# Memory rows and riding rows by DMA in place of selection matmuls, with a fixed TensorE order, in a recurrent attention and gated-MLP kernel

## The chip, the core and the metric

The kernel runs on one core of one Trainium2 chip. The core has five instruction queues: TensorE (PE, matmuls, with its weight loads shown as PEld), VectorE (DVE), ScalarE (ACT), GpSimd (POOL) and SyncE (SP), which issues nearly all DMAs here. The engines run side by side and wait for one another through semaphores. The metric is the device time of one execution in microseconds, lower is better; the number given is the median of several executions.

## What is computed

Two rounds of the same pair of residual blocks over x of 2048 rows by 448, in bfloat16:

```python
x = x + A(layernorm(x));  x = x + B(layernorm(x))
x = x + A(layernorm(x));  x = x + B(layernorm(x))

def A(x, mem):                      # 64 segments of 32 rows, one after the other
    for s in range(64):
        h = concat([mem, x[32*s:32*s+32]])          # 8 memory rows + 32 rows = 40
        q, k, v = h @ Wq, h @ Wk, h @ Wv            # 16 heads of 256
        p = softmax(mask(q @ k.T / 16))             # every row sees the memory rows
        o = (p @ v) @ Wo
        mem = o[:8]                                 # the next segment's memory
        out.append(o[8:])
def B(x):                           # ReGLU: 448 -> 1792 -> 448
    return (relu(x @ W_gate) * (x @ W_up)) @ W_down
```

The memory makes A a recurrence: segment s+1 can't begin its queries of the memory rows before segment s has its eight new ones.

## The kernel before

**Algebra.** A setup of about 72 us folds the weights: for each head, M = Wq·Wk transposed (448 by 448) and N = Wv·Wo (448 by 448), both kept in SBUF (`Mw`, `M3`, `Nw`). A head's scores are then h·M·h transposed, and its output is p·h·N. The 448 columns are cut into three chunks of 128 and one of 64, so 16 heads make 56 blocks of N.

**Steps.** The two rounds (layer 0 and layer 1) are interleaved with a lag of four segments: step t, for t from 0 to 67, does segment t of layer 0 and segment t-4 of layer 1 in the same instructions where it can (one half of the partitions, or one half of the columns, for each). A step consists of these groups, named as in the code:

- `m_nat`: brings the new memory rows in natural layout into hK; also moves the "riding" rows (below)
- `t_block`: h·M for all heads (three blocks of matmuls; the copies out are `t_copies`, into TTm for the memory queries and TTs for the segment queries)
- `s_mem`, `p_t_mem`, `u_mem`, `un_mem`: scores, softmax, transposed probabilities, p·h (copied into UTm) and ·N for the memory rows; the result is `mv`, which holds the new memory rows and, in a second set of 16 columns of its window, rows that came along
- `m_t`: the new memory rows, transposed, into hT (the keys of the next step)
- `s_seg`, `seg_pt`, `u_seg`: the same for the 32 segment rows; the transposed probabilities PTs come by a transposing DMA
- every second step `un` (·N, and the residual into XB), `ln_b` with a transposing DMA to xBT, `b_layer` and `b_down` (the MLP), and `ln_a`, with a transposing DMA to xAT, for a later pair of segments

hK holds h in natural layout (rows on partitions): 32 segment rows and 8 memory rows for each layer and each of four slots. `u_mem` and `u_seg` read it, over all 40 rows. "Riding" rows are the segment rows of one layer-1 segment that went through `un_mem` beside the memory rows, in columns of UTm; they come out in `mv` and have to be added into the residual XB, 16 rows at a time.

**How mv gets where it is needed, before.** `mv` has 64 rows of 224 columns: the two column halves of 32 result rows. `m_nat` (L1207) does two matmuls with 0/1 matrices `seln`, prepared in setup (L712, L730), which put the rows onto the partitions at which hK, and the riding rows, are wanted; hK is then copied out of PSUM (L867 on ScalarE or L868 on VectorE), and the riding rows go into XB in two VectorE additions, one in each of two steps (L1225 into part, L1228 into XB). `m_t` does 14 small matmuls with `selm`, one VectorE copy and two ScalarE copies into hT.

**What sets the order.** All operations are recorded first (`_Order.add`), with what they read and write. `_Order.run` then lays them out on the five queues: whenever an engine is free in its account, it takes, among the operations that can start soonest, the one with the highest priority. The priority of a TensorE group comes from a table, `SLOT` (L174), by name, index and step: steps 0 to 3 and 64 to 67 have entries of their own, the steps between share one set for each step number modulo four, shifted by `PERIOD`. Other operations take theirs from what depends on them, plus `BIAS` (L164). The result is a fixed order on each engine, and every engine executes its queue in order; waits are added in `_Sched._need` (L69). Four steps with t % 4 = 0 to 3 are called a group of four here, and its first to fourth step.

**Tile shapes.** Matmuls here use TensorE whole (128 rows by 128 columns), in quarters of 64 by 64, or in column groups of 32, and the order decides how often the shape changes from one group to the next. A group with `alt=2`, such as m_nat, may be issued whole or in four column groups, whichever fits its neighbour.

Of the kernel before, what the change touches and what calls it, by code (L numbers as in the profile page):

```python
# [9 lines left out]
ALU = mybir.AluOpType  # L10
AX = mybir.AxisListType

D = 448
# [3 lines left out]
MEM = 8  # L17
SEG = 32
KEYS = SEG + MEM

NSEG = 64
# [3 lines left out]
DH = D // 2  # L25
# [4 lines left out]
LAG = 4  # L30
# [15 lines left out]
class _Sched:  # L46
# [118 lines left out]
    "t_blockm+": 5039, "t_blocks+": 3092, "s_mem+": -5347, "p_t_mem+": -85965, "u_mem+": -33073, "un_mem+": -7892,  # L165
    "un_memh+": -922, "m_t+": -4047, "m_tk+": 22842, "s_seg+": -67106, "seg_pt+": 139, "u_seg0+": -1085,
    "u_seg1+": -443, "u_seg2+": -2585, "u_seg3+": 51857, "m_nat+": 3185, "t_block0f+": 662, "t_block0r+": 9055,
    "t_block1r+": 5367, "t_block2r+": 47616, "ln_a+": 3189, "ln_ac+": -12510, "un+": -111, "ln_b+": -12694,
    "b_layer+": -12996, "b_down+": -5101, "m_natx+": -272, "stay": 46, "win": 118,
# [5 lines left out]
    "t_block0f.0@a0": 38481, "t_block0r.0@a0": 67520, "t_block0r.1@a0": 67619, "t_block0r.2@a0": 67659,  # L175
    "t_block0r.3@a0": 67621, "t_block0r.4@a0": 67623, "t_block0r.5@a0": 70316, "t_block1f.0@a0": 38479,
    "t_block1r.0@a0": 67656, "t_block1r.1@a0": 65565, "t_block1r.2@a0": 67536, "t_block1r.3@a0": 67536,
    "t_block2r.0@a0": 74464, "s_mem.0@a0": 47525, "fills_mem.0@a0": 48698, "fills_mem.1@a0": 46922,
    "p_t_mem.0@a0": 67621, "u_mem.0@a0": 57404, "fillu_mem.0@a0": 48642, "un_mem.0@a0": 45458, "m_t.0@a0": 45462,
    "s_seg.0@a0": 67571, "u_seg0.0@a0": 57410, "u_seg1.0@a0": 57412, "u_seg2.0@a0": 53498, "u_seg3.0@a0": 57450,  # L180
    "m_nat.0@a1": 45460, "t_block0f.0@a1": 48668, "t_block0r.0@a1": 46927, "t_block0r.1@a1": 46927,
    "t_block0r.2@a1": 46949, "t_block0r.3@a1": 46923, "t_block0r.4@a1": 46925, "t_block0r.5@a1": 46921,
    "t_block1f.0@a1": 41930, "t_block1r.0@a1": 47860, "t_block1r.1@a1": 46934, "t_block1r.2@a1": 45772,
    "t_block1r.3@a1": 49346, "t_block2r.0@a1": 42010, "s_mem.0@a1": 46933, "fills_mem.0@a1": 46935,
    "fills_mem.1@a1": 46937, "p_t_mem.0@a1": 46939, "u_mem.0@a1": 55586, "fillu_mem.0@a1": 47077,
    "un_mem.0@a1": 45464, "m_t.0@a1": 45504, "s_seg.0@a1": 46931, "u_seg0.0@a1": 57408, "u_seg1.0@a1": 57416,
    "u_seg2.0@a1": 57443, "u_seg3.0@a1": 61660, "un0.0@a1": 45416, "un0.1@a1": 45474, "un0.2@a1": 45706,
    "un0.3@a1": 86975, "un1.0@a1": 45440, "un1.1@a1": 45442, "un1.2@a1": 88746, "un1.3@a1": 86915, "un2.0@a1": 89373,
    "un2.1@a1": 86931, "un2.2@a1": 45626, "un2.3@a1": 45444, "un3.0@a1": 45669, "un3.1@a1": 47005,
    "b_layerf.0@a1": -26914, "b_layer.0@a1": 46812, "b_layer.1@a1": 46814, "b_layerf.1@a1": 46769,  # L190
    "b_layer.2@a1": 46810, "b_layer.3@a1": 46826, "b_down.0@a1": 44084, "b_down.1@a1": 44185, "b_down.2@a1": 47906,
    "b_down.3@a1": 47908, "b_down.4@a1": 47910, "b_down.5@a1": 47912, "b_down.6@a1": 47914, "m_nat.0@a2": 59501,
    "t_block0f.0@a2": 20916, "t_block0r.0@a2": 59499, "t_block0r.1@a2": 59503, "t_block0r.2@a2": 59507,
    "t_block0r.3@a2": 59497, "t_block0r.4@a2": 45282, "t_block0r.5@a2": 59135, "t_block1f.0@a2": 48655,
    "t_block1r.0@a2": 59518, "t_block1r.1@a2": 59522, "t_block1r.2@a2": 59520, "t_block1r.3@a2": 59516,
    "t_block2r.0@a2": 48355, "s_mem.0@a2": 41082, "p_t_mem.0@a2": 44080, "u_mem.0@a2": 76553, "un_mem.0@a2": 45624,
    "m_t.0@a2": 45632, "s_seg.0@a2": 59497, "u_seg0.0@a2": 76181, "u_seg1.0@a2": 87512, "u_seg2.0@a2": 76188,
    "u_seg3.0@a2": 48788, "m_nat.0@a3": 70659, "t_block0f.0@a3": 47001, "t_block0r.0@a3": 46830,
    "t_block0r.1@a3": 46838, "t_block0r.2@a3": 46828, "t_block0r.3@a3": 46832, "t_block0r.4@a3": 46836,
    "t_block0r.5@a3": 46834, "t_block1f.0@a3": 47003, "t_block1r.0@a3": 48603, "t_block1r.1@a3": 48556,  # L200
    "t_block1r.2@a3": 48562, "t_block1r.3@a3": 48560, "t_block2r.0@a3": 47673, "s_mem.0@a3": 49023,
    "p_t_mem.0@a3": 46824, "u_mem.0@a3": 48389, "un_mem.0@a3": 47916, "m_t.0@a3": 47902, "s_seg.0@a3": 47542,
    "u_seg0.0@a3": -27897, "u_seg1.0@a3": -26535, "u_seg2.0@a3": -26849, "u_seg3.0@a3": -26851, "un0.0@a3": 47904,
    "un0.1@a3": 47906, "un0.2@a3": 47908, "un0.3@a3": 47910, "un1.0@a3": 44845, "un1.1@a3": 61780, "un1.2@a3": 47816,
    "un1.3@a3": 47939, "un2.0@a3": 47830, "un2.1@a3": 47904, "un2.2@a3": 47948, "un2.3@a3": 47820, "un3.0@a3": 48725,
    "un3.1@a3": 47900, "b_layerf.0@a3": -26847, "b_layer.0@a3": 132467, "b_layer.1@a3": 132469,
    "b_layerf.1@a3": -26849, "b_layer.2@a3": 132473, "b_layer.3@a3": 132471, "b_down.0@a3": 36585,
    "b_down.1@a3": 49933, "b_down.2@a3": 47822, "b_down.3@a3": 47832, "b_down.4@a3": 46594, "b_down.5@a3": 39676,
    "b_down.6@a3": 47861, "m_nat.0@0": 450296, "t_block0f.0@0": 6985, "t_block0r.0@0": 20136, "t_block0r.1@0": 20140,
    "t_block0r.2@0": 190863, "t_block0r.3@0": 20138, "t_block0r.4@0": 190282, "t_block0r.5@0": 192142,  # L210
    "t_block1f.0@0": 108960, "t_block1r.0@0": 190290, "t_block1r.1@0": 104286, "t_block1r.2@0": 190288,
    "t_block1r.3@0": 104284, "t_block2r.0@0": 190292, "s_mem.0@0": 20286, "p_t_mem.0@0": 20493, "u_mem.0@0": -63618,
    "un_mem.0@0": -180079, "m_t.0@0": -438077, "s_seg.0@0": 100996, "u_seg0.0@0": -60148, "u_seg1.0@0": -65797,
    "u_seg2.0@0": 363822, "u_seg3.0@0": 26075, "m_nat.0@1": -268008, "t_block0f.0@1": 108464, "t_block0r.0@1": 278134,
    "t_block0r.1@1": 106489, "t_block0r.2@1": 192798, "t_block0r.3@1": 278136, "t_block0r.4@1": 278138,
    "t_block0r.5@1": 273223, "t_block1f.0@1": 17227, "t_block1r.0@1": 192130, "t_block1r.1@1": 192132,
    "t_block1r.2@1": 106130, "t_block1r.3@1": 192132, "t_block2r.0@1": 106128, "s_mem.0@1": -151868,
    "p_t_mem.0@1": -65864, "u_mem.0@1": -28209, "un_mem.0@1": 311409, "m_t.0@1": 192901, "s_seg.0@1": 106134,
    "u_seg0.0@1": 22464, "u_seg1.0@1": 57795, "u_seg2.0@1": 57793, "u_seg3.0@1": 195218, "un0.0@1": 139411,
# [310 lines left out]
def MM(out, lhsT, rhs, **kw):  # L530
    return (out, lhsT, rhs, kw)
# [921 lines left out]
```

## Time and profile before

| | us |
|---|---|
| median of three runs | 1547.75 |
| lowest, highest | 1545.5, 1551.47 |
| the profiled execution | 1548.94 |
| its span, first to last instruction | 1547.1 |
| VectorE busy by DVE copies of TTs, 64x256 and 128x320 | 43.0 + 28.8 |
| ScalarE busy by copies of TTs, 128x320 | 129.7 |
| POOL busy | 111.8 |
| ACT copies into hT, 64x16 (118 of them) | 21.3 |

The page gives, for each engine, busy time and share of the span, a digit row in 40 slices, the chain of work that ended last, and groups of instructions. A group's line has the source line, engine, operation, the tile it writes and the tiles it reads, the count, and then busy time in all, mean duration in ns, and the idle time of the engine just before, with what ended it. Nearly all operations go through helpers, so L139 is every matmul, L867 every ScalarE copy and L868 every copy on VectorE or GpSimd; the tiles tell them apart. Matmuls overlap in the pipeline, so the distance between starts, and not the duration, is what one costs.

The DMA part of the page, for the transfers that are issued inside the steps (KB each, median us from issue to landing; the transposing ones have no size):

```
out_dram<-ys SPq DMA_DIRECT2D x32, 56.0 KB, 2.1
XA<-in_A_x_dram SPq DMA_DIRECT2D x28, 56.0 KB, 2.2
PTs<-Ps SPq DMA_TRANSPOSE x67, 2.6
xBT<-xn SPq DMA_TRANSPOSE x34, 3.2
```

### The profile page before, as it was taken

How to read it: one execution, taken by the hardware profiler on the slowest of the kernel's cores; microseconds unless marked ns; L12 is line 12 of the kernel's file. 1: busy time of each engine (PE TensorE's matmuls, PEld its weight loads, DVE VectorE, ACT ScalarE, POOL GpSimd, SP SyncE). 2: the span in 40 equal slices, each digit the busy share in tenths (PEclk: the TensorE clock that was granted, in tenths of full speed). 3: DMA queues.
4: the chain of work that ended last, by engine and by line, in shares of the span. 5: the costliest groups of instructions: out<-in, count | busy, mean ns of one | idle time of the engine just before them, and what ended most of it. 6: DMA issues, size and time to landing. Idle time of an engine off the chain costs nothing.

```text
span 1547.1 us, 87788 instructions
## 1 busy us (share of the span) xinstructions
PE 1489.5 (96%) x40831; PEld 1173.4 (76%) x40835; DVE 826.2 (53%) x2213; ACT 865.0 (56%) x2780; POOL 111.8 (7%) x259
## 2 busy tenths in 40 slices
PE   6989999999999999999999999999999999999998
PEld 2568777778787777878687778878777787878776
DVE  6434545555554655554564554555465555556445
ACT  5745554655555565555556465554656556555543
POOL 4000000000000000000000000000000000000000
PEclk9999999999999999999999999999999999999999
DMA  9841111000010101000010110001010111101010
GB/s 216 185 124 26 19 14 21 19 15 17 20 21 15 22 15 20 17 15 21 15 22 15 20 20 15 17 20 21 15 22 16 20 16 16 19 15 19 19 19 15
DMA packets 129757, 46.37 MB, mean 30 GB/s; under 512 B 117736, under 2 KB 129264, under 8 KB 129392
## 3 DMA queue, kind: packets, MB, share of 16 engines
q1 hardware_dynamic: 129040, 40.53, 13.6%
q8 instruction: 320, 5.24, 1.4%
q14 instruction: 45, 0.37, 0.1%
q10 hardware_dynamic: 352, 0.24, 0.1%
HBM read 10.33 MB, written 1.84 MB: 8 GB/s over the span
## 4 chain that ended last, share of the span: by engine, by line
PE 86%; ACT 4%; DVE 4%; DMA 3%; SPq 3%; issue 1%
PE b L139 86%; SPq L688 3%; DMA PTs<-Ps 2%; ACT TTs L867 1%; ACT UTm L867 1%; ACT Em L1072 1%; ACT big L867 1%; DMA xBT<-xn 1%; DVE stat L1116 1%; ACT TTm L867 0%; ACT Es L1115 0%; DMA Nw<-in_A_Wo_dram 0%; DVE UTm L868 0%; DVE Es L1114 0%; DVE xn L921 0%
## 5 line engine op out<-in xcount | busy, mean ns | idle before, releaser
L139 PE MATMUL b<-hT,Mw 128*128 128x80 bf16 (+1 forms) x11424 | 439.5, 200 | 0.6 <-issue 0.3
L139 PEld LDWEIGHTS b<-hT,Mw 128*128 128x128 bf16 x11424 | 418.7, 100 | 14.8 <-issue 1.8
L139 PE MATMUL b<-Nw,big 128*32 128x448 bf16 (+1 forms) x3324 | 294.5, 353 | 0.6 <-DMA Nw<-in_A_Wo_dram 0.5
L867 ACT ACTIVATE TTs<-b 128x320 bf16<-128x320 f32 (+5 forms) x676 | 282.1, 418 | 22.1 <-PE b L139 20.5
L867 ACT ACTIVATE TTm<-b 128x80 bf16<-128x80 f32 (+5 forms) x660 | 152.7, 232 | 181.6 <-PE b L139 175.8
L139 PE MATMUL b<-Nw,UTm 128*32 128x224 bf16 x7504 | 196.2, 262 | 17.2 <-DVE UTm L868 15.8
L139 PEld LDWEIGHTS b<-Nw,big 128*32 128x32 bf16 (+1 forms) x3324 | 133.7, 97 | 102.5 <-issue 5.8
L139 PE MATMUL b<-xBT,big 128*128 128x128 bf16 (+3 forms) x4900 | 209.5, 215 | 1.0 <-DVE xn L921 0.6
L139 PEld LDWEIGHTS b<-Nw,UTm 128*32 128x32 bf16 x7504 | 177.9, 98 | 35.7 <-DVE UTm L868 18.0
L139 PEld LDWEIGHTS b<-xBT,big 128*128 128x128 bf16 (+1 forms) x4900 | 183.2, 101 | 21.1 <-issue 8.2
L867 ACT ACTIVATE big<-b 128x512 bf16<-128x512 f32 (+1 forms) x250 | 125.4, 559 | 85.5 <-PE b L139 84.5
L139 PE MATMUL b<-hT,M 64*64 64x80 bf16 (+2 forms) x6808 | 144.1, 199 | 2.7 <-issue 1.3
L868 DVE CAST TTm<-b 64x64 bf16<-64x64 f32 (+4 forms) x224 | 49.7, 223 | 176.0 <-PE b L139 172.6
L139 PEld LDWEIGHTS b<-hT,M 64*64 64x64 bf16 (+2 forms) x6808 | 109.6, 107 | 28.3 <-ACT hT L867 11.2
L868 POOL COPY hK<-xn 32x448 bf16<-32x448 bf16 x136 | 75.2, 553 | 624.9 <-DVE xn L921 618.6
L1350 ACT ACTIVATE gT<-b 128x512 bf16<-128x512 f32 (+2 forms) x128 | 67.8, 541 | 63.7 <-PE b L139 58.0
L868 DVE CAST TTs<-b 64x256 bf16<-64x256 f32 (+5 forms) x208 | 88.9, 428 | 20.0 <-PE b L139 19.8
L139 PE MATMUL b<-big,hB 128*32 128x448 bf16 (+1 forms) x742 | 95.2, 353 | 0.5 <-DVE hB L1351 0.4
L1351 DVE TENSOR_TENSOR hB<-gT,b 128x512 bf16<-128x512 bf16 (+2 forms) x128 | 78.3, 614 | 28.3 <-PE b L139 14.4
L867 ACT ACTIVATE UTm<-b 128x448 bf16<-128x448 f32 (+2 forms) x132 | 73.3, 566 | 33.8 <-PE b L139 33.8
L867 ACT ACTIVATE sumA<-b 64x224 f32<-64x224 f32 x67 | 23.7, 354 | 122.0 <-PE b L139 122.0
L139 PE MATMUL b<-PTs,hK 40*64 40x512 bf16 (+1 forms) x1024 | 83.5, 364 | 6.5 <-DMA PTs<-Ps 6.5
(109 smaller groups left out, 1509.0 us busy)
## 6 DMA issues: line engine op xcount, KB each, us to landing
big<-in_A_Wo_dram SPq DMA_DIRECT2D x3, 896.0 KB, 5.9
out_dram<-ys SPq DMA_DIRECT2D x32, 56.0 KB, 2.1
big<-in_B_W_up_dram SPq DMA_DIRECT2D x7, 224.0 KB, 3.1
big<-in_B_W_gate_dram SPq DMA_DIRECT2D x7, 224.0 KB, 4.1
big<-in_B_W_down_dram SPq DMA_DIRECT2D x7, 224.0 KB, 2.7
XA<-in_A_x_dram SPq DMA_DIRECT2D x28, 56.0 KB, 2.2
PTs<-Ps SPq DMA_TRANSPOSE x67, 2.6
Nw<-in_A_Wo_dram SPq DMA_DIRECT2D x1, 896.0 KB, 6.1
```

Of the source, the lines that this page charges most:

```text
L139: ins = E.matmul(out, lhsT=lhsT, rhs=rhs, **kw)
L688: S.q.add("dma", ("sp",), {"sp": 6200.0 if w == "Wv" and q else 4100.0}, lambda E: E.dma_start_transpose(out=st[w, q], in_=src[w][:, q * 1 ...
L867: return E.activation(out(), src(), ACT.Copy, **({} if scale is None else {"scale": scale}))
L868: return E.tensor_copy(out(), src()) if scale is None else E.tensor_scalar(out(), src(), scale, None, op0=ALU.mult)
L1072: S.act(lambda E, i=i: E.activation(S.Em[:, i, :], src()[:, i, :], ACT.Exp, bias=st[:, 32 + i:33 + i], scale=1.0, accum_out=st[:, 34 + i:3 ...
L1116: S.dve(lambda E: E.tensor_reduce(st[:, 48:48 + n], Es, AX.X, ALU.add), w, [("Es",)], [("ss", 1)])
L1350: S.act(lambda E, g=g, R=R, n=n: E.activation(S.gT[:, g, 0:n], R[0].b()[:, 0:n], ACT.Relu), n, R[0].res(), [("gT", g)])
L1351: S.dve(lambda E, g=g, R=R, n=n, fcs=fcs: E.tensor_tensor(S.hB[:, fcs[0]:fcs[-1] + 1, 0:w], S.gT[:, g, 0:n].rearrange("p (a b) -> p a b", ...
```

## The change

1. `m_nat` has no matmul and no PSUM tile any more. The memory rows go from `mv` into hK by DMA on SP, one for each layer and column half (four per step), and the riding rows by two more DMAs into a new tile `ride`. In every second step one VectorE addition (ride + XA into XB) takes the place of the two. `seln` and its setup are gone.
2. `m_t` does 16 matmuls instead of 14, so that all 128 partitions of the last chunk are filled, and one VectorE copy into hT takes the place of three.
3. After the priorities are worked out, all TensorE groups of steps 8 to 63 that have a `SLOT` entry are sorted by it and chained one to the next, so that the plan must keep that order. The chain is in the plan alone and adds no waits.
4. `SLOT` and `BIAS` have new numbers throughout, and a cost allowance of 60 ns in `s_mem` is dropped in the plan.

```diff
@@ _Order.graph
             o.prio = -o.key
+        line = sorted((o for o in self.ops if o.slot in SLOT and 2 * LAG <= o.t < NSEG), key=lambda o: o.key)
+        for a, b in zip(line, line[1:]):
+            if a not in b.preds:
+                b.preds.append(a)
+                b.np += 1
+                a.succs.append(b)
@@ alloc
-        self.seln = self.sb("seln", [128, 2, 2, 128])
+        self.ride = self.sb("ride", [128, D])
@@ m_t
-                for g in range(4) if c < 3 else (2, 3):
-                    d = 128 * c + 32 * g - (64 if c == 3 else 0)
+                for g in range(4):
+                    d = 128 * c + 32 * (g if c < 3 else g % 2)
...
-        S.cp(lambda: S.hT[:, pp, 0:3, l0:l1, s, SEG:KEYS], lambda: v()[:, 0:3], 48, C.res(), mk[:-2], eng=("dve",))
-        S.cp(lambda: S.hT[0:64, pp, 3, l0:l1, s, SEG:KEYS], lambda: v()[64:128, 3], 16, C.res(half=(1,)), mk[-2:-1], eng=("act",), base=(64, 0))
-        S.cp(lambda: S.hT[64:128, pp, 3, l0:l1, s, SEG:KEYS], lambda: v()[64:128, 3], 16, C.res(half=(1,)), mk[-1:], eng=("act",), base=(64, 64))
+        S.cp(lambda: S.hT[:, pp, :, l0:l1, s, SEG:KEYS], lambda: C.b()[:, 0:64].rearrange("p (c l q) -> p c l q", c=4, l=2)[:, :, l0:l1, :], 64, C.res(), mk, eng=("dve",))
@@ m_nat
-        S.mm(lambda: [MM(C.b()[:, DH * j:DH * j + DH], S.seln[:, j, w, :], S.mv[:, :], start=True, stop=True) for j in range(2)],
-             2 * S.pitch(DH), [("mem",), ("sel", 0), ("sel", 1)], C.res() + [("hKm", pp, s, l) for l in ls], alt=2)
-        for l in ls:
-            r = slice(64 * l + 32, 64 * l + 40)
-            S.cp(lambda r=r: S.hK[r, pp, s, :], lambda r=r: C.b()[r, 0:D], D, C.res(half=(l,)), [("hKm", pp, s, l)], base=(r.start, r.start))
+            for n in range(2):
+                a, b = 64 * l + 32, 32 * n + 16 * w + 8 * l
+                S.qdma(f"mk{l}{n}", lambda E, a=a, b=b, n=n: E.dma_start(S.hK[a:a + 8, pp, s, DH * n:DH * n + DH], S.mv[b:b + 8, :]),
+                       [("hKm", pp, s, l, n)], [("mem",)])
...
-            if w == 0:
-                S.dve(lambda E: E.tensor_tensor(S.part[r, :], C.b()[r, 0:D], S.XA[r, p % 4, :], ALU.add), D,
-                      C.res(half=(1,)) + [("XA", p % 4, 1)], [("part", 1)], base=(64, 64))
-            else:
-                S.dve(lambda E: E.tensor_tensor(S.XB[r, (p + 1) % 2, :], C.b()[r, 0:D], S.part[r, :], ALU.add), D,
-                      C.res(half=(1,)) + [("part", 1)], [("XB", (p + 1) % 2, 1)], base=(64, 64))
+            for n in range(2):
+                a, b = 64 + 16 * w, 32 * n + 16 * (1 - w)
+                S.qdma(f"ride{n}", lambda E, a=a, b=b, n=n: E.dma_start(S.ride[a:a + 16, DH * n:DH * n + DH], S.mv[b:b + 16, :]), [("ride", w, n)], [("mem",)])
+            if w == 1:
+                S.dve(lambda E: E.tensor_tensor(S.XB[r, (p + 1) % 2, :], S.ride[r, :], S.XA[r, p % 4, :], ALU.add), D,
+                      [("ride", i, n) for i in range(2) for n in range(2)] + [("XA", p % 4, 1)], [("XB", (p + 1) % 2, 1)], base=(64, 64))
```

`qdma` records a DMA on SP's queue. `u_mem` and `u_seg` now read the memory rows of hK under two keys (one for each column half), so they wait for the DMAs that write them. In the programs as built, SP's queue has 376 more DMAs: 252 into hK and 124 into ride.

## The prediction

> **What bounds the kernel now.** I read the page first, then the windows by stage, the waits of TensorE, the groups by shape, and the timeline where TensorE stands still.
>
> ```profile
> span 1547.1 us, 87788 instructions
> ...
> PE 1489.5 (96%) x40831; PEld 1173.4 (76%) x40835; DVE 826.2 (53%) x2213; ACT 865.0 (56%) x2780; POOL 111.8 (7%) x259
> ...
> PEclk9999999999999999999999999999999999999999
> ...
> PE 86%; ACT 4%; DVE 4%; DMA 3%; SPq 3%; issue 1%
> ```
>
> TensorE is busy 96% of the span at full clock, and 86% of the chain that ended last is its own. VectorE and ScalarE are half idle. So a microsecond counts only if it leaves TensorE's queue or is a moment in which TensorE waits. The windows (length, then busy time of PE, PEld, DVE, ACT, POOL, clock, DMA share, GB/s) say where those moments are:
>
> ```profile
> 0.00:80.00 80.00, 61.70 (x672) 32.13 (x675) 45.67 (x149) 52.46 (x154) 18.67 (x32) 0.98 0.91 197
> 80.00:255.00 175.00, 162.77 (x4942) 132.07 (x4940) 85.41 (x248) 90.13 (x314) 9.25 (x24) 0.95 0.19 41
> 255.00:1490.00 1235.00, 1213.15 (x33679) 970.60 (x33677) 668.49 (x1749) 700.47 (x2237) 81.04 (x196) 1.00 0.10 18
> 1490.00:1548.00 58.00, 51.93 (x1552) 38.59 (x1552) 26.62 (x69) 21.96 (x78) 2.86 (x7) 1.00 0.08 17
> ```
>
> Setup ends near 72 us, steps 0 to 7 near 215 us; then come 14 like groups of four steps of 88.4 us each (from un_mem to un_mem in the trace). From 255 to 1490 us only 21.9 us are idle. The waits name them (total, times, longest):
>
> ```profile
> PE b L139 <- DVE UTm L868: 15.8, 15, 1.2
> ...
> PE b L139 <- DMA PTs<-Ps: 6.5, 8, 2.8
> PE b L139 <- DVE mv L1179: 3.7, 10, 0.9
> ...
> PE b L139 <- DVE Pm L1076: 2.8, 3, 1.2
> ```
>
> UTm is the large one: once in four steps.
>
> **Part 1, the selection matmuls.** The removed groups (busy, mean ns | idle before):
>
> ```profile
> L867 ACT ACTIVATE hK<-b 8x448 bf16<-8x448 f32 x111 | 59.5, 536 | 35.1 <-PE b L139 19.4 <-DVE part L1225 8.7 <-DVE XB L1228 4.7
> L1225 DVE TENSOR_TENSOR part<-b,XA 32x448 f32<-32x448 f32 x31 | 19.3, 622 | 8.5 <-PE b L139 7.9
> L139 PE MATMUL b<-mv,seln 128*128 128x224 bf16 x90 | 16.0, 260 | 0.0
> L139 PE MATMUL b<-mv,seln 128*32 128x224 bf16 x176 | 8.5, 257 | 1.0 <-DVE mv L1179 0.9
> ```
>
> The two seln rows add to 24.5 us of busy time. The Trainium skill ("Trainium Kernel Development and Optimization", Performance Expectations) calls matmul busy time a bad metric because matmuls are pipelined. Here that decides the sum, so I read start times instead:
>
> ```profile
> 837.81 0.35 PE L139 MATMUL b<-mv,seln 128*128 128x224 bf16 x2
> 838.00 2.06 PE L139 MATMUL b<-Nw,big 128*128 128x448 bf16 x10
> ```
>
> The next matmul starts 0.19 us after the first of m_nat. 67 calls x 0.19 = **-12.7 us**, not -24.5. The copies leave engines that have room: ScalarE loses 111 x 0.536 = 59.5 us, VectorE 31 x 0.622 + 15 x 0.628 = 28.7 us; worth nothing by themselves, only where they stood ahead of something TensorE waits for (part 4). The seln set-up (L712, L730) ends by about 9.4 us, while TensorE's first work waits 8.4 us for the DMA ys<-in_A_mem_dram: 0.
>
> **Part 2, m_t.** 16 matmuls for 14. A timeline row of the 14 lasts 0.27 us and one lasts 0.17, so 13 starts take 0.10, 0.008 each: 67 x 2 x 0.008 = +1.1. One VectorE copy of 64 columns for three copies (48 on VectorE, 0.20 us; two on ScalarE, 0.18 each): 0, nothing waits there now.
>
> **Part 3, the order: shape changes.** The built programs show TensorE's order. From step 8 on before repeats a group of 172 TensorE operations per four steps with 51 changes of tile shape; after repeats one of 168 with 45. What a change costs:
>
> ```profile
> 802.69 0.73 PE L139 MATMUL b<-hT,M 64*64 64x80 bf16 x60
> 803.36 0.71 PE L139 MATMUL b<-hT,Mw 128*128 128x80 bf16 x15
> ```
>
> The last 64*64 matmul starts at 802.69 + 0.73 - 0.20 = 803.22, the first 128*128 at 803.36: 0.14 against 0.036 inside the group, so about 0.095 us. 14 x 6 x 0.095 = **-8.0 us**. Outside steps 8 to 63 after has 9 changes more: +0.9.
>
> **Part 3, the order: the stall at UTm.**
>
> ```profile
> 830.47 0.37 PE L139 MATMUL b<-PTm,hK 40*64 40x128 bf16 x16
> ...
> 831.19 0.61 DVE L868 CAST UTm<-b 128x448 bf16<-128x448 f32 x1
> ...
> 831.87 2.87 PE L139 MATMUL b<-Nw,UTm 128*32 128x224 bf16 x112 [1.03 <-DVE UTm L868]
> ```
>
> In the fourth step of a group un_mem follows u_mem with nothing between, and waits for the copy into UTm: 1.03 us idle, 1.09 counted from when it could have started. After puts u_seg3 (0.11), a shape change with b_down chunk 5 (0.48) and chunk 6 (0.38) there: 0.97 us, so 0.12 stays. 14 x 0.97 = **-13.6 us**. Next late is PTs: u_seg of the same step waits for a transpose issued when Ps is done. Counted from that, TensorE has as much queued as before (stall replaced by work), so the 6.5 us stay: 0.
>
> **Part 4, smaller stalls.** m_t of the fourth step waits for mv (3.7 in all): after puts four u_seg pieces (0.89 us) before it instead of two (0.56). Pm (2.8) waited in the third step, where the m_nat copies ran just ahead of the softmax on both engines. Of 6.5 us I take **-4.0** (ends 0 and -6.5). Against it: without m_nat (0.19) TensorE reaches b_layer sooner and may wait for xBT, and in the first step of a group only 0.55 us stand between m_t and the next t_block, where a free VectorE needs about 0.4 and one in a 0.68 us cast more. 2 x 0.1 x 14 = +2.8 (ends 0 and +8). Steps 0 to 7 (12.2 us idle from 80 to 255): steps 4 and 5 lose cover (in step 5 p_t_mem, u_mem, un_mem and m_t follow one another directly), the rest is mixed: +3 (ends -3 and +8).
>
> **Part 5, the added DMAs and waits.** 252 transfers of mv rows to hK and 124 to ride, six per step, all on SP. The Trainium skill ("DMA: Bandwidth & Descriptors", Rules for kernel authors) speaks against this: coalesce, since under 64 KB one pays mostly overhead; these hold 3.6 or 7.2 KB. The nearest row is the load of XA (56 KB): 0.47 us of SP, landed 2.2 us after issue. If each paid its landing in turn, the sixth would land 13 us after mv; by the row, issues overlap: 5 x 0.47 + 2.2 = 4.6 us. hK is next read by u_mem of the next step, behind all of t_block (7.5 us), s_mem and the softmax: over 9 us later. By the row 0, by the strict reading over 3 us in each of 63 steps, +190. The row shows issues of 0.47 us, so 0. On SP nothing urgent stands behind the six: the next items are x, xBT or PTs, due a t_block or an LN later. TensorE gets about five more waits a step (four on u_mem, with the whole step queued behind). The trace has operations with none to three satisfied waits: un or s_seg gain 0 to 5 ns from one to the next. 359 x 0.0025 = +0.9 (ends 0 and +18, at 50 ns). ride is read by one VectorE add in every second step, with that step's TTm and TTs copies queued behind it. At its tighter place it comes about 3.2 us after mv, and ride lands at 0.47 + 2.2 = 2.7: 0.
>
> **Sum.** -12.7 + 1.1 - 8.0 + 0.9 - 13.6 - 4.0 + 2.8 + 3.0 + 0.9 = -29.6. The profiled execution took 1548.94 us (span 1547.1), so 1519.3; the median of the runs, 1547.75, is 1.2 lower, so **1518 us**. The likeliest case alone spans 1507 to 1528. The rivals are counted from the median too.
>
> **Rivals.** (a) *Only the counts go.* The stalls move: TensorE, early at every later wait, pays the UTm and mv microseconds at PTs and xBT. For: PTs transposes land 2.4 to 4 us after issue, and its cover is fixed by Ps. Against: the 0.97 us put into the gap is work that stood elsewhere in the queue, where no wait follows it. -12.7 + 1.1 - 8.0 + 0.9 + 3.0 + 0.9 = -14.8: 1533. (b) *Slower: VectorE stands at the ride add.* The chain of waits shows a transfer in the same queue that takes long:
>
> ```profile
> 831.30 3.97 DMA PTs<-Ps
> ```
>
> If every ride lands 4.5 us after its issue instead of 2.2, the add is 1.8 us late in each of 28 odd steps, the t_block copies stand behind it, and banks run out: 28 x 1.8 = +50, 1568. It decides above 2.2 + 0.5 + 29.6/28 = 3.8 us in every such step. Against: copies of 56 KB have a median of 2.2. (c) *More goes*: PTs and Pm waits vanish too, steps 0 to 7 gain: 1502. That the order isn't kept is excluded: after's order has the same 45 changes in each group.
>
> **Numbers.** Forecast 0.66, (a) 0.18, (b) 0.05, (c) 0.11. The range 1504 to 1537 holds the forecast, most of (a) and half of (c). No change (within 0.5%, 7.7 us, about what can be measured) needs three quarters of the gain to fail: 0.03. Faster 0.91, slower 0.06.
>
> **What would show it.** Right: no mv,seln row; groups of four steps of about 86.1 us instead of 88.4; the wait for UTm under 3 us; u_mem not waiting for a DMA into hK; PTs waits still 4 to 9 us. Wrong: a VectorE wait on DMA ride in the list of waits, TensorE waits on hK, or u_mem growing by over 0.1 us with its five waits.

## The result, and the profile after

The changed kernel takes 1536.15 us (median of four runs, 1534.62 to 1539.28) against 1548.99 us for the kernel before in the same comparison: a ratio of 0.9921 [0.9895, 0.9948]. Measured again later on another chip it was 0.9941 [0.992, 0.9962]. So it is 0.6 to 0.8% faster, 9 to 13 us, where 29.6 were forecast. The profiled execution took 1535.5 us.

The page of the kernel after, its head and its chain of waits, then the windows (length, busy time of PE, PEld, DVE, ACT, POOL, clock, DMA share, GB/s) and rows of the waits (total, times, longest):

```profile
span 1533.6 us, 88464 instructions
...
PE 1477.1 (96%) x41047; PEld 1157.1 (75%) x41051; DVE 803.6 (52%) x2198; ACT 777.2 (51%) x2491; POOL 112.8 (7%) x259
...
PE 83%; DVE 5%; DMA 4%; SPq 3%; ACT 3%; issue 1%
```

```profile
255.00:1477.00 1222.00, 1202.71 (x33965) 959.22 (x33967) 647.08 (x1725) 628.39 (x2011) 81.94 (x196) 1.00 0.11 20
1477.00:1535.00 58.00, 49.55 (x1475) 36.24 (x1477) 26.25 (x76) 18.33 (x63) 2.93 (x7) 0.99 0.09 17
```

```profile
DVE XB L1221 <- DMA ride<-mv: 18.2, 19, 1.7
...
PE b L139 <- issue: 5.2, 13, 0.7
PE b L139 <- ACT UTm L864: 5.0, 16, 0.9
PE b L139 <- DMA xBT<-xn: 4.0, 5, 1.3
PE b L139 <- DMA PTs<-Ps: 3.1, 7, 0.6
PE b L139 <- DVE Pm L1073: 3.0, 4, 1.2
PE b L139 <- DVE mv L1176: 2.5, 5, 0.9
```

TensorE has 12.4 us less to do (1489.5 before), and its wait for UTm is down from 15.8 us (for VectorE's copy) to 5.0 (for ScalarE's). Yet from 255 us on it still stands still for 19.3 us (21.9 before), and in the last 58 us for 8.4 (6.1 before). Three rows are new or grown: xBT (0.3 before), *issue*, which is a wait that ends with nothing the profile shows (1.9 before), and on VectorE the wait for ride.

These rows mix all stages. To follow every TensorE operation from kernel to kernel, I took the times at which TensorE reports the end of each operation, and from the distance of each to the one before subtracted its undisturbed length: the plan's own number for it, and 0.095 us where the tile shape changes. What is left over is time in which it was held up. So the row of undisturbed work is a count, and the others are what was measured beyond it. The sums for steps 8 to 63, and the stages around them, all from profiled executions, us ("2nd steps" are those with t % 4 = 1; the texts on record for x2 and x9, below, call the same t_block that of the first step):

```
                                before  after    x1     x3     x6     x7     x8
setup                             71.7   71.6   73.2   71.2   71.7   73.7   71.4
steps 0 to 7                     143.7  142.7  143.9  143.2  146.2  142.3  142.2
steps 8 to 63                   1238.1 1220.3 1233.0 1218.2 1216.3 1228.1 1213.4
  undisturbed work              1207.3 1188.5 1196.5 1188.5 1188.5 1196.6 1188.5
  held up: un_mem, 4th steps      15.1    4.5   15.2    4.5    4.5   15.2    4.5
  p_t_mem (Pm)                     2.2    3.6    3.6    3.6   -0.2   -0.2   -0.2
  u_seg, m_t, un0, 4th steps       7.8    8.8    8.0    8.9    8.8    7.7    8.8
  first of b_layer (xBT)           1.4    4.1    2.4    1.5    3.6    3.4    1.5
  t_block of 2nd steps             0.4    4.0    1.1    4.6    3.7    0.6    4.2
  t_block of the others            0.7    3.1    1.9    2.8    3.3    0.8    2.3
  the rest                         3.2    3.5    4.2    3.8    4.2    4.1    3.9
tail, after un_mem of step 63     93.6   99.0   94.4  100.9   98.0   96.9   96.3
```

The undisturbed work fell by 18.8 us, and un_mem gave 10.6. Against these gains stand 1.4 (Pm), 1.0, 2.7 (xBT), 3.6 and 2.4 (t_block), and 5.4 in the tail. That the rest stays at 3.2 to 4.2 in all kernels says that the undisturbed lengths, the 0.095 us among them, fit; and where nothing waits, the trace's own lengths agree with the plan's: a piece of un 0.378 us against 0.379, of t_block 0.537 against 0.539, a group of b_layer 0.670 against 0.671. A second profile of the changed kernel gave 1223.8 us for steps 8 to 63 instead of 1220.3, so a total of one profile can't tell less than about 4 us. The rows for un_mem and Pm repeat to 0.1 us, xBT gave 4.1 and 5.0, t_block of the 2nd steps 4.0 and 5.8.

The stages around steps 8 to 63 hold one thing more. In every profile TensorE's granted clock is 0.5 for some stretches of 3.4 or 6.8 us, nearly all of them before step 8 or in the tail (in x9 one reaches 0.2 us into step 8). In steps 0 to 7 these come to 17.1 us in the kernel before and 10.2 us in the changed one. In the tail before has none and the changed kernel one. The windows below are of before, after, before and after; the clock is the third number from the end:

```profile
72.00:215.00 143.00, 129.44 (x4066) 105.51 (x4069) 67.67 (x203) 69.59 (x248) 9.05 (x23) 0.94 0.23 52
```

```profile
72.00:215.00 143.00, 129.00 (x4058) 102.71 (x4056) 68.47 (x211) 62.38 (x218) 9.07 (x23) 0.96 0.22 52
```

```profile
1454.00:1547.00 93.00, 86.95 (x2493) 65.56 (x2491) 43.02 (x119) 40.20 (x152) 4.85 (x13) 1.00 0.10 17
```

```profile
1456.00:1459.00 3.00, 3.00 (x72) 2.51 (x64) 0.00 (x0) 0.00 (x0) 0.00 (x0) 0.50 0.24 44
1459.00:1533.00 74.00, 67.55 (x2000) 51.30 (x1990) 36.10 (x107) 26.19 (x90) 3.11 (x8) 1.00 0.09 17
```

Half the length of such a stretch is my estimate of what it costs while TensorE has work. Why the stretches fall where they do is not shown here.

### The profile page after: what moved, and what is told of

The parts are those of the page before. It is cut to its first block, busy times and chain, and to the rows that moved or that the text cites. A ratio compares the mean times of both kernels' runs of the same rounds, so it can differ in the third digit from the quotient of the medians.

```text
span 1533.6 us, 88464 instructions
## 1 busy us (share of the span) xinstructions
PE 1477.1 (96%) x41047; PEld 1157.1 (75%) x41051; DVE 803.6 (52%) x2198; ACT 777.2 (51%) x2491; POOL 112.8 (7%) x259
## 4 chain that ended last, share of the span: by engine, by line
PE 83%; DVE 5%; DMA 4%; SPq 3%; ACT 3%; issue 1%
PE b L139 83%; SPq L690 3%; DMA PTs<-Ps 2%; DVE big L865 1%; DMA xBT<-xn 1%; ACT UTm L864 1%; ACT Em L1069 1%; DVE UTm L865 1%; DMA xAT<-xn 1%; SPq L1211 1%; DMA ride<-mv 0%; DVE mv L1176 0%; DVE Es L1111 0%; DMA Nw<-in_A_Wo_dram 0%; ACT sumA L864 0%
## 5 line engine op out<-in xcount | busy, mean ns | idle before, releaser
L864 ACT ACTIVATE TTm<-b 128x80 bf16<-128x80 f32 (+5 forms) x639 | 149.2, 234 | 273.8 <-PE b L139 266.1
L864 ACT ACTIVATE TTs<-b 128x320 bf16<-128x320 f32 (+5 forms) x640 | 269.0, 420 | 5.3 <-PE b L139 4.9
L865 DVE CAST TTm<-b 64x64 bf16<-64x64 f32 (+4 forms) x245 | 54.6, 223 | 200.1 <-PE b L139 196.0
L139 PE MATMUL b<-hT,M 64*64 64x80 bf16 (+3 forms) x6808 | 145.9, 199 | 2.3 <-DVE hT L865 1.4
L864 ACT ACTIVATE big<-b 128x512 bf16<-128x512 f32 (+1 forms) x228 | 111.1, 544 | 60.8 <-PE b L139 60.4
L865 DVE CAST big<-b 128x512 bf16<-128x512 f32 (+1 forms) x160 | 97.3, 624 | 64.0 <-PE b L139 63.3
L864 ACT ACTIVATE UTm<-b 128x512 bf16<-128x512 f32 (+2 forms) x173 | 87.2, 541 | 64.8 <-PE b L139 64.0
L865 DVE CAST TTs<-b 64x256 bf16<-64x256 f32 (+5 forms) x244 | 102.6, 420 | 5.4 <-PE b L139 5.4
L139 PE MATMUL b<-big,hB 128*128 128x448 bf16 (+1 forms) x574 | 100.0, 353 | 0.8 <-DVE hB L1343 0.8
```

The lines of the kernel that those rows point to most:

```text
L139: ins = E.matmul(out, lhsT=lhsT, rhs=rhs, **kw)
L864: return E.activation(out(), src(), ACT.Copy, **({} if scale is None else {"scale": scale}))
L865: return E.tensor_copy(out(), src()) if scale is None else E.tensor_scalar(out(), src(), scale, None, op0=ALU.mult)
```

## The experiments

My theory A at the start: the six transfers are not free, because SP needs 0.6 us for each issue, so that VectorE stands at the ride add and xBT comes late. Theory B: the transfers are free and the stalls of the order only moved. All times against the kernel before on the same chip:

| run | median us | ratio |
|---|---|---|
| x1_dma_old_order | 1546.24 | 0.9978 [0.997, 0.9987] |
| x2_ride_add_later | 1543.45 | 0.995 [0.9931, 0.9969] |
| x3_sp_order | 1532.24 | 0.9896 [0.9877, 0.9915] |
| x4_old_tail | 1533.19 | 0.9895 [0.988, 0.991] |
| x5_utm_copy_first | 1537.88 | 0.9936 [0.9915, 0.9957] |
| x6_softmax_first | 1532.7 | 0.9895 [0.9877, 0.9913] |
| x7_dma_old_order_softmax | 1542.73 | 0.9966 [0.9952, 0.9979] |
| x8_all_four | 1527.78 | 0.986 [0.9845, 0.9874] |
| x9_shift_packets | 1544.27 | 0.9932 [0.991, 0.9953] |
| x10_all_four_shifted | 1528.78 | 0.9845 [0.9826, 0.9864] |
| x11_after_again | 1543.73 | 0.9941 [0.992, 0.9962] |
| x12_three | 1531.05 | 0.9863 [0.9841, 0.9884] |

In all of them TensorE's order is written out as a list and chained from the first step to the last, so that an edit elsewhere can't move it:

```diff
-        line = sorted((o for o in self.ops if o.slot in SLOT and 2 * LAG <= o.t < NSEG), key=lambda o: o.key)
+        line = sorted((o for o in self.ops if o.slot and o.t in LINE.get(o.slot.rsplit("@", 1)[0], {})), key=lambda o: LINE[o.slot.rsplit("@", 1)[0]][o.t])
...
```

**The two halves: x1 and x7.** LINE holds the order of the kernel before without m_nat; x7 also changes one priority (see x6).

> The changed code (DMAs into the keys and into ride, m_t of 16 matmuls), but TensorE's whole order is that of the kernel before, with m_nat taken out. Theory A (the six transfers are not free: SP needs about 0.6 us for each issue, so VectorE stands at the ride add and xBT comes late): less is gained than the matmuls give, -12.7 + 1.1 for the counts and about 3 to 7 us back, 1540 to 1544 us, with VectorE waiting for ride. Theory B (the transfers are free, and it is the new order whose stalls only moved): the counts alone, about 1537 us, and no wait for ride that TensorE feels. In both the UTm wait stays near 15 us, since the old order leaves nothing between u_mem and un_mem.

> The transfers in the order of the kernel before, as in x1_dma_old_order, with the max of the softmax ahead of the second copy of u_seg0 in the fourth step, as the kernel before has it. If the transfers themselves cost nothing (my part 5), what x1 lacked was that place on VectorE: steps 8 to 63 fall from 1233.0 by 3.8 to about 1229, which is 9 us under before, as the counts say, and the whole to 1542. If the transfers cost (late ride and xBT, theory A), the steps stay within 1 us of 1233.

x1 gained 3.0 us, less than A had it. But of what x1 lacks, 3.8 us sit at one place, p_t_mem of the fourth steps, which has nothing to do with a transfer, and x7 took them away: steps 8 to 63 fell to 1228.1, 10.0 under before. Undisturbed work alone gives 10.7. The waits are not all as before, though: xBT rose by 2.0, t_block and the rest by 1.1, while the Pm row lost 2.4, since the copies that ran ahead of the softmax in the third step are gone. So in the old order the six transfers cost TensorE at most about 3 us in 56 steps, 2.0 of them at xBT. Outside these steps x7 gives back another 3.9: +2.0 in the setup, -1.4 in steps 0 to 7, +3.3 in the tail (see x4). The new order gives the rest: from x1 to the changed kernel, steps 8 to 63 lose 12.7 us.

**VectorE's wait for ride: x2.** The plan is told that a ride transfer needs longer, so the add stands later in VectorE's queue.

```diff
-    def qdma(self, name, fn, wr, rd=()):
-        self.q.add("dma", ("sp",), {"sp": 500.0}, fn, rd, wr, name=name)
+    def qdma(self, name, fn, wr, rd=(), cost=500.0, lat=None):
+        self.q.add("dma", ("sp",), {"sp": cost}, fn, rd, wr, name=name, lat=lat)
@@ m_nat, the ride transfers
-[("ride", w, n)], [("mem",)])
+[("ride", w, n)], [("mem",)], lat=5000.0)
```

> The changed kernel with TensorE's order kept; only the plan is told that a ride transfer needs 2.8 us longer, so the ride add comes later in VectorE's queue (the plan's rules, not the chip, move it). Theory A: VectorE's wait for ride (18.2 us before) falls to under 3 us, the t_block matmuls of every first step of a group lose their 0.2 us waits, and 3 to 6 us are gained: 1530 to 1533. xBT stays late. Theory B (TensorE's waits have nothing to do with the ride add): the wait for ride goes, the time stays within 1 us of 1536.

The wait of 18.2 us is gone, all of it, and steps 8 to 63 took 1220.6 us instead of 1220.3: within the 4 us that a profile can tell, the wait cost nothing there. VectorE stood, and nothing that TensorE waited for stood behind it. This half of theory A fell. The time, though, fits neither theory: the ratio of 0.995 lies above the interval of the changed kernel's first measurement (up to 0.9948) and inside that of its second. The profile of x2 has 2.7 us more in steps 0 to 7 and 5.1 more in the tail than the changed kernel's. Most of this is the granted clock: it is 0.5 for 17.1 us in steps 0 to 7 and 10.2 in the tail, against 10.2 and 3.4, which by half the difference is 6.8 of the 7.8 us. Whether the later add has a part in that stays open.

**SP's queue: x3.** Here is what the changed kernel does on SP once in four steps (timeline; start, length, engine, line, operation):

```profile
1024.92 2.64 SPq L1211 DMA_DIRECT2D hK<-mv  x4
...
1027.60 1.63 SPq L1218 DMA_DIRECT2D ride<-mv  x2
...
1029.28 0.58 SPq L829 DMA_DIRECT2D XA<-in_A_x_dram  x1
...
1029.90 1.27 SPq L977 DMA_TRANSPOSE xBT<-xn  x1
...
1030.41 0.38 DVE L1221 TENSOR_TENSOR XB<-ride,XA 32x448 bf16<-32x448 bf16 x1 [1.16 <-DMA ride<-mv]
...
1034.08 0.64 PE L139 MATMUL b<-xBT,big 64*64 64x128 bf16 x32 [0.63 <-DMA xBT<-xn]
```

An issue into hK takes 0.63 us and one of ride 0.59 (medians), not the 0.47 that the row of XA gave. Six fill SP for 4.3 us here, and behind them stand XA and then the transpose xBT, which is issued the moment SP is free, though its input was ready 0.6 us before. The edit puts ride first and XA behind xBT:

```diff
+        for o in self.ops:
+            if o.kind == "dma" and o.name.startswith("ride"):
+                o.prio += 1e6
+        xb = {o.t: o for o in self.ops if o.name == "xBT"}
...
+        for o in self.ops:
+            if o.name in ("x0", "x1", "x2", "x3") and o.cat == "un" and o.t in xb and xb[o.t] not in o.preds:
+                o.preds.append(xb[o.t])
...
```

> The changed kernel with TensorE's order kept; on SP the two ride transfers go ahead of the four into hK in every step, and the load of XA goes behind the transpose xBT. Theory A: ride lands 1.2 + 1.8 = 3.0 us after mv instead of 5.1, ahead of the add at 4.4, and xBT is issued 0.2 to 0.9 us earlier; the wait for ride falls under 4 us and b_layer's first group loses its mean wait of 0.3 us: 14 x (0.25 + 0.3) = 7 to 8 us, 1528 to 1531. Theory B: under 2 us. Theory C (landings of transposes take 2.4 to 4.2 us whatever stands ahead of them): xBT waits stay, and only the ride part comes, 1532 to 1534.

In the fourth steps xBT is now issued 3.50 us after un ends, as soon as xn is ready, in all but one group (3.67 to 4.51 us in the changed kernel, but for one). The two waits in x3:

```profile
PE b L139 <- DMA xBT<-xn: 0.2, 1, 0.2
```

```profile
DVE XB L1315 <- DMA ride<-mv: 7.2, 8, 1.7
```

The xBT row falls from 4.1 to 1.5. It is 1.5, 1.7 and 2.4 in x8, x10 and x12, which have the same order on SP, and 3.6 to 7.3 in the seven profiles with the changed kernel's. The t_block row of the 2nd steps does not fall, as x2 had shown, and VectorE's wait is 7.2 us, not under 4. So theory A is right for xBT, 2.6 us here, and for nothing more; the time, 1532.24, came out where C had it. C's mechanism fell in part: the wait went with the order on SP alone, but where it stands also hangs on the late landings (x9).

Against the kernel before, SP is only part of the story. There xBT was issued 3.92 us after un ended, as late as in the changed kernel on the average (3.91), where xn is ready sooner and SP takes the time back. But before, TensorE had 8.03 us of undisturbed work between un and b_layer in these steps, and now it has 7.71, and xBT landed 3.48 us after its issue before and 4.01 after (medians of the 13 fourth steps, 11 to 59). That is the shorter cover of the prediction's part 4; x3 got it back by issuing sooner.

**The softmax: x6.** VectorE in the fourth step, before and after (the last row of each is TensorE's first weight load of p_t_mem):

```profile
1004.38 0.69 DVE L868 CAST UTm<-b 128x512 bf16<-128x512 f32 x1 [0.97 <-PE b L139]
1004.99 0.23 DVE L1070 TENSOR_REDUCE stat<-b 128x2 f32<-128x80 f32 x1
1005.14 0.68 DVE L868 CAST big<-b 128x512 bf16<-128x512 f32 x1
...
1007.02 0.10 PEld L139 LDWEIGHTS b<-ident,Pm 128*128 128x128 bf16 x1 [0.26 <-DVE Pm L1076]
```

```profile
992.14 0.69 DVE L865 CAST UTm<-b 128x512 bf16<-128x512 f32 x1 [1.51 <-PE b L139]
...
992.75 0.68 DVE L865 CAST big<-b 128x512 bf16<-128x512 f32 x1
...
993.34 0.23 DVE L1067 TENSOR_REDUCE stat<-b 128x2 f32<-128x80 f32 x1
...
995.06 0.10 PEld L139 LDWEIGHTS b<-ident,Pm 128*128 128x128 bf16 x1 [0.54 <-DVE Pm L1073]
```

Before, the max (TENSOR_REDUCE) stood between the two copies of u_seg0; after, both copies are ahead of it, and Pm comes 0.28 us later. That is the new BIAS table, seen on VectorE.

```diff
-    "s_mem+": -350,
+    "s_mem+": -5000,
```

> The changed kernel, TensorE's order kept. In the fourth step VectorE copies two pieces of u_seg0 (0.6 us each) before the max of the memory softmax; before it stood between them. Here the max goes ahead of the second copy, and one copy of u_seg0 changes places with one of u_seg2 between VectorE and ScalarE. Theory D (the retuned priorities put a copy ahead of the softmax): p_t_mem of the fourth step loses its wait of 0.27 us, 14 x 0.27 = 3.8 us, 1532. Theory E (the wait moves on to UTm, PTs or mv, which hang on the same chain): the 0.27 us turn up at un_mem, u_seg0 or m_t of the same step, under 1 us.

The Pm row went from 3.6 to -0.2 and nothing rose in its place: theory D. E would have shown at un_mem, u_seg or m_t, which stay at 4.5 and 8.8.

**un_mem: x5.**

```diff
-    "u_mem+": -471,
+    "u_mem+": -20000,
```

> The changed kernel, TensorE's order kept. In the fourth step of a group u_seg3 was moved into the gap between u_mem and un_mem, and its own copy (0.27 us) runs on ScalarE ahead of the copy into UTm; here the copy into UTm goes first (one priority changed). Theory D (the moved piece brings its eviction along, ahead of the very copy that un_mem waits for): un_mem's excess falls from 0.32 to 0.1 us, 14 x 0.2 = 3 us, 1533. Theory E (what un_mem gains is waited for at the next late thing, u_seg0 and m_t, whose inputs PTs and mv do not come sooner): un_mem's excess falls, u_seg0 and m_t of the same step rise by as much, and the time stays within 1 us of 1536.

A miss for both. ScalarE does take the copy of u_mem first (its end is 0.86 us after u_mem instead of 1.14), and un_mem's excess stays at 0.32. The two timelines, after and then x5:

```profile
996.06 1.31 ACT L864 ACTIVATE UTm<-b 128x512 bf16<-128x512 f32 x3 [0.46 <-PE b L139]
...
997.42 2.87 PE L139 MATMUL b<-Nw,UTm 128*32 128x224 bf16 x112 [0.24 <-ACT UTm L864]
```

```profile
994.57 1.31 ACT L947 ACTIVATE UTm<-b 128x512 bf16<-128x512 f32 x3 [0.46 <-PE b L139]
...
995.93 2.87 PE L139 MATMUL b<-Nw,UTm 128*32 128x224 bf16 x112 [0.24 <-ACT UTm L947]
```

Three copies in a row on ScalarE write into the tile UTm: that of u_seg1 first, then those of u_seg3 and u_mem in either order. un_mem starts 0.05 us after the end of the last (996.06 + 1.31 = 997.37; 994.57 + 1.31 = 995.88), in whichever order they come. The code says why: the riding segment rows lie in UTm too (`home` returns `UTm[:, :, 16:48]` in even steps), and un_mem reads `("UW", c)` for all four chunks. The u_seg3 that the new order moved into the gap is that of the third step, an even one, and writes chunk 3. It fills the gap and lengthens the wait that the gap is for. In x5 the two copies of u_mem are done by 995.69 (VectorE's, the later one); with the same 0.05 us un_mem could have started at 995.74 and not 995.93, which would leave 0.13 of the 0.32 us, an estimate. No run took u_seg3 out of the gap.

**The tail: x4.** LINE is the changed order up to un_mem of step 63, then that of the kernel before without m_nat.

> The changed kernel; after the un_mem of step 63 TensorE's remaining work is in the order of the kernel before (without m_nat), all before that as it was. The tail took 93.6 us before and 99.0 after. If the changed order of the tail costs the 5.4 us, it falls to about 94 less four m_nat (0.8) and the time to 1530; if the DMAs cost it (last steps have less work to cover a transfer), the tail stays at 98 to 99 and the time within 1 us of 1536.

The tail took 96.5 us, and 96.3, 97.0 and 97.9 in x8, x10 and x12, which have the same one; with the changed order it was 98.0 to 104.1 in seven profiles, 99.0 in the middle. In the changed kernel un of step 63 lies wholly before step 64, since the chain ends at step 63 and holds un ahead of everything that follows; s_mem, p_t_mem, u_mem and un_mem of step 64 then come with only s_seg between, held up for 4.2 us in all. Some 2.1 us of that are waits, and 1.6 are un_mem itself, which falls into the stretch of half clock (4.48 us for its usual 2.87):

```profile
1454.66 0.38 PE L139 MATMUL b<-PTm,hK 40*64 40x128 bf16 x8 [0.32 <-DVE PTm L865]
1455.68 4.48 PE L139 MATMUL b<-Nw,UTm 128*32 128x224 bf16 x112 [0.64 <-ACT UTm L864]
```

With the old tail the first group of b_layer waits for xBT instead, 2.0 to 2.7 us in x1, x4, x7, x8, x10 and x12, and not at all in the kernel before: that is where the transfers cost something in the tail. With half of each stretch of half clock taken off (an estimate), the tail is 97.0 to 99.0 us in the seven profiles with the changed order, 97.5 in the middle, 94.4 to 95.3 in the six with the old one, and 93.6 before, which still has four m_nat (0.8). So of the 5.4 us about 2.8 are the order, 1.7 the clock, and the transfers cost 1.6 to 2.5, against the 0.8 that m_nat gave.

**t_block of the 2nd steps: x9 and x10.** In these steps TensorE stands still with *issue* as the reason, in a few groups only:

```profile
590.46 0.41 PE L139 MATMUL b<-hT,Mw 128*128 128x80 bf16 x7 [0.28 <-issue]
...
594.31 1.21 PE L139 MATMUL b<-hT,Mw 128*128 128x80 bf16 x29 [0.48 <-issue]
```

The page lists a queue of instructions, 323 packets of 16 KB; 82,098 matmuls and weight loads make 254 for each. The packets around these two waits:

```
start 587.70, took 1.44 us   landed 589.14   TensorE goes on at 590.46, 1.32 us later
start 591.71, took 1.28 us   landed 592.99   TensorE goes on at 594.30, 1.31 us later
```

The other waits agree: all 11 of TensorE's *issue* waits over 0.08 us between 215 and 1434 us end 1.26 to 1.50 us after a packet has landed, and so do, within 1.22 to 1.60, all 53 of x8 to x11, though packets are 4.3 us apart (median). So TensorE seems to have run out of instructions. If so, the place of these waits hangs on how packets and program fall together, and 128 instructions more at the start must move them:

```diff
+        T2 = S.tile("R", 1)
+        S.mm(lambda: [MM(T2.b()[:, 0:8], S.ident[:, :], S.ident[:, 0:8], start=True, stop=True) for _ in range(64)], 1600.0, [("ident",)], T2.res())
         S.start_mem(0)
```

> The changed kernel with 64 tiny matmuls more (128 instructions with their weight loads) in a gap of the setup in which TensorE stands still anyway; they write a bank that nobody reads. The trace shows TensorE's instructions coming in packets of 16 KB, one in about 4 us, and its unexplained waits in t_block of the first step of a group (4 us in all, in steps 21 to 33 only) end 1.3 us after such a packet has landed. Theory F (TensorE runs out of instructions there; where, is set by how the packets fall): 128 instructions are half a packet, so the waits leave steps 21 to 33 and turn up in steps 37 to 55, whose packets were 2 us later; sum and time stay, 1536 within 3 us. Theory G (the waits belong to the work of these steps): they stay in steps 21 to 33.

> The kernel of x8_all_four with the same 64 tiny matmuls. Theory F: the t_block waits move as in x9, and the late xBT and PTs transposes move to other groups too, since they also land 1.0 to 1.6 us after a packet of instructions; 1528 within 3 us. Theory G: nothing moves.

They moved. In the changed kernel the t_block waits of the 2nd steps lie in steps 21 to 33 (besides one in step 9, which every kernel with the new order has), in its second profile, x11, in 13 to 37; in x9 they lie in steps 45 to 61, later than the 37 to 55 I gave, with the same sum of 4.0 us. In x8 they are in steps 13 to 37, in x10 nearly all in 45 to 61. The waits at u_seg0 for PTs moved as well, from steps 39 to 59 to steps 11 to 31, and from x8's 47 to 63 to x10's 15 to 35. The waits for xBT moved from steps 35 to 51 to steps 11 to 39, with a sum of 7.3 us for 4.1, and the t_block waits of the other steps moved and rose from 3.1 to 6.1, so x9's profile has 1226.1 us for steps 8 to 63, and not all sums stayed. Theory F, for the place. The ratios stayed (0.9932 and 0.9845), on a chip where the kernel before took 1553.42; the 1544.27 us of x9 are 8 over the text on record. The kernel before has 0.4 us there, and x1 and x7 1.1 and 0.6 with all the transfers and the old order: what brings these waits about is the new order. It leaves three pieces of un (0.38 us each, 4 instructions) between the u_seg pieces and t_block where the old one has six, so TensorE comes to the quick stretch with fewer in hand. That last sentence is argued; no run changed it alone.

**All together: x8, x11, x12.** x8 has the edits of x3, x4, x5 and x6, x12 those of x3, x4 and x6; x11 is the changed kernel again beside x12.

> All four edits on the changed kernel: ride ahead of hK and XA behind xBT on SP, the copy into UTm ahead of u_seg3's, the max of the softmax ahead of the second u_seg0 copy, and the old order of the tail. If the waits are separate they add up: 4 + 3 + 3.8 + 3 = 14 us under 1536, 1522, near the time I forecast for the change alone. If they are one chain (theory E), only the SP and tail parts come, 1529. Over 1531: the edits are in each other's way.

> The changed kernel once more, on the same chip as the next one, its order written out as a list instead of computed from the tables (the same program). 0.992 of the kernel before, as it was; under 0.989 or over 0.995 would say that single runs of it differ by more than the effects I am sorting out.

> The three edits that did something (ride ahead of hK and XA behind xBT on SP, the max of the softmax ahead of the second u_seg0 copy, the old order of the tail), without the edit of x5. If x5 does nothing also here: 0.986 of the kernel before, 6 to 10 us under the changed kernel beside it; if it matters in company, 0.988.

x8 is at 0.986 [0.9845, 0.9874], 21 us under the kernel before and 8 to 9 under the changed one. That is not the 1522 of waits that add up and a little under the 1529 of one chain; x3, x4 and x6 alone had gained 3.9, 3.0 and 3.5 us, 10.4 together, so they nearly add up, at smaller sizes than I had given them. x12 lies 12.7 us under x11 by the medians of the same chip, with a ratio of 0.9863 as x8 has: the edit of x5 does nothing in company either. By the table 3.8 of this are Pm, 2.6 xBT, 2 to 3 the tail; what is left, 3 to 4, has no cause shown; it is no more than two profiles of one kernel differ by.

```profile
span 1523.3 us, 88273 instructions
...
PE 1473.8 (97%) x40951; PEld 1157.4 (76%) x40955; DVE 802.7 (53%) x2198; ACT 775.0 (51%) x2491; POOL 112.3 (7%) x259
```

## Why the prediction was right or wrong

The direction was right and the time of 1536.15 lies inside the range, near its upper end; the gain is 12.8 us where 29.6 were forecast. Two steps failed most: part 4, which took -4.0 from the smaller stalls and +2.8 from shorter cover and got +2.4 and +8.7, and the tail, to which it gave no stall. The waits at UTm, mis-sized by 3.0, come third. That the range held the time is owed to its width, and not to the sum. By its steps, in us of the profiled executions:

- **m_nat, m_t and the shape changes: right.** Forecast for steps 8 to 63: -10.6 + 0.9 - 8.0 = -17.7. The count above gives -18.8 without the 0.9 of m_t, and the measured times leave the rest where it was (3.2 before, 3.5 after). In the trace of before m_nat takes 0.192 us from end to end (median); m_t with 16 matmuls takes 0.159 us for 0.143, the 2 x 0.008 of the sum. Counting starts, and not the 24.5 us of busy time, was what made this hold.
- **The stall at UTm: mechanism right, size off.** -13.6 was forecast, -10.6 came, since 0.32 us stay and not 0.12. The failed term is "so 0.12 stays": I took u_seg3 as cover, and un_mem also waits for what u_seg3 writes (read in the code and the timelines of x5). The wait for UTm is 5.0 us, not under 3 as the prediction's sign had it.
- **The smaller stalls, -4.0: wrong.** The waits for Pm in the third steps did go (2.4 us to 0), but the new table puts a copy ahead of the max in the fourth step, and 0.27 us x 14 = 3.8 came there (x6). The gain at mv was paid back: m_t lost 1.5 us of its wait (3.1 to 1.6) and u_seg0 0.8, but u_seg3 and un0 of the same step rose by 1.5 and 2.0, and the row went from 7.8 to 8.8. The failed step is the sum's reading that a wait with more work put before it is gained in full. What u_seg3 and un0 wait for there stays open.
- **The cover of xBT and t_block, +2.8: too small by 5.9.** xBT +2.7, t_block +6.0. For xBT part 4 named the right cause, less cover, and took it as 0.1 us a group: 0.32 us went in the fourth steps, and the landing was 0.5 us longer. And part 5 failed with "On SP nothing urgent stands behind the six": the row of XA gave 0.47 us for an issue, these take 0.63 and 0.59, and xBT, which I named as due an LN later, is due just as they end. Setting that right gave 2.6 us back (x3). The t_block waits stand where TensorE seems to be out of instructions, for which the sum had no term (x9); in half of the groups t_block of the 2nd step is not held up at all, so the copy on VectorE that part 4 named is no steady cost there.
- **The added transfers and waits, 0 and +0.9: nothing found for the waits, 2 to 3 us short for the transfers.** In the old order these cost TensorE at most about 3 us in steps 8 to 63, 2.0 of it at xBT (x7). u_mem takes 0.340 us with one wait and with five. The sign that I had named as "wrong", a VectorE wait for ride, did appear, 19 times, 18.2 us; where four issues into hK went ahead of ride on SP, the add came 4.4 us after mv and ride landed at 5.1, and not 2.7 against 3.2. But it was no sign of loss (x2). Rival (b) had the place right and the price wrong.
- **Outside steps 8 to 63.** Steps 0 to 7 were forecast at +3.0 before m_nat's share and came at -1.0 in all. That is in part luck: the clock was at half for 6.8 us less in the changed kernel's profile, 3.4 us by the estimate. The "full clock" of the prediction's first part was 0.94 in this stage. The tail had only its count of shape changes, and gave back 5.4: the order, a stretch of half clock and xBT of step 63 (x4).

Rival (a), 1533, came nearest to the time, and its words "the stalls move" describe the sum but not the place: the UTm gain stayed a gain, PTs paid little of it, and waits that the forecast had too small or not at all took the place of it, at xBT, at Pm, in t_block and in the tail. That its number came so near is in part luck.

## What to carry to other kernels

A piece of work that is moved into a gap brings along what it reads and writes and its own evictions: look whether the operation after the gap reads what the piece writes. When many small transfers are added, price them by the time the issuing queue is taken, item by item, against the next urgent item on that queue; a wait that appears on an engine with room is not a loss until something is shown to stand behind it. When an order is fixed for the steady part, read its edges, and every other engine's queue at the places that the old order had tuned. And before a difference between two profiles is put down to an edit, compare their granted clock stage by stage.

## What the runs showed of the hardware

- Instructions arrive in 16 KB packets during the run, one in about 4 us, and all 64 of TensorE's *issue* waits in five kernels end 1.2 to 1.6 us after one has landed, most of them in stretches where 80-column matmuls leave every 36 ns. Where this happens shifts with the number of instructions ahead (x9).
- The transposing transfers are late when such a packet is under way. In the kernel before, from 215 to 1477 us, a transpose landed 2.41 us after its issue, and never over 2.53, when no packet of instructions was under way between 1.0 us after the issue and the landing (19 of PTs, 7 of xBT, medians), and 3.40 (38 of PTs) and 3.63 us (21 of xBT) when one was; 47 of these 59 landed 1.0 to 1.6 us after the packet had. With the packets shifted, the waits for PTs and xBT moved (x9). So the "2.4 to 4 us" of PTs is for the most part this.
- A transfer of 3.5 or 7 KB inside SBUF takes SP 0.63 or 0.59 us to issue, more than the load of 56 KB from DRAM (0.47 in the kernel before, 0.53 in the changed one).
- The granted clock of TensorE drops to half for 3.4 or 6.8 us at a time, in these kernels before step 8 and in the tail. One such stretch made an un_mem take 4.48 us for 2.87.
